# Local attention into a gated FFN: scores of both heads in row halves, and five PSUM banks shared by scores and V products

## The chip, the cores and the metric

One core of a Trainium2 chip. The metric is the device time of one execution in microseconds. TensorE (PE) multiplies into PSUM, ScalarE (ACT) and VectorE (DVE) read PSUM, GpSimd (POOL) works in SBUF and issues some of the DMAs, and SyncE (SP) issues the others. Each engine has its own list of instructions, and they wait for each other by semaphores.

## The reference

Attention with a local window of 96 keys and 8 global keys, then a gated FFN over all heads' outputs:

```python
scores = scale * q @ k.T                      # batch 4, heads 8, seq 768, head_dim 64
keep = (pos_k < 8) | ((rel >= 0) & (rel < 96))
dist = where(is_global & ~is_local, 96, abs(rel))
scores = where(keep, scores - slopes[h] * dist, -1e9)
a = exp(scores - max); a = a / (sum(a) + 1e-9)
x = (a @ v), heads side by side               # 3072 x 512
out = (maximum(x @ w_gate, 0) * (x @ w_val)) @ w_out   # 512 -> 1536 -> 512, float32
```

## The kernel before

**Halves and chunks.** The sequence of each batch is cut into two halves of 384 queries, so there are eight halves `s` = 0 to 7. Half `s` goes through attention, which leaves `xT` (512 features by 384 tokens), and chunk `c` = `s` of the FFN takes it from there. Halves 0 and 1 have code of their own (`scores`, `masks`, `first_sums` and so on); halves 2 to 7 are the "later halves", made by `attention_pieces`. Chunks 2 to 7 form the output product with seven products in place of eight for two of their three token tiles (`block`, sums in DVE).

**Attention of a later half**, for each of four head pairs `p` (two heads lie on the two halves of the 128 partitions):

- `early_pieces(s)`: POOL casts the loaded keys and queries to bf16 (`piece_cast_k`, `piece_cast_q`), SP issues transposing DMAs (`piece_xk` to `kN`, `piece_xq` to `qT`), and POOL puts the keys into steps of 128 (8 global and 120 local keys, `piece_order` with `put_keys`: three copies for each pair).
- Queries are padded: `qz` has, for each head, the head's 64 features and 64 zeros, so that `qT` holds both heads on all 128 rows and one product of 128 rows gives the scores of both heads side by side. Its zeros are written once (`Z`).
- `piece_qk(s, p, g)`, three for each pair: the scores of a group of key steps into one bank (`psum["qk"]`, three banks), an exp on ACT into `es`, and the mask products on DVE (L420).
- `piece_av(s, p, e)`, one for each head: V products into one bank (`psum["av"]`, two banks, L436); the same product with ones gives the sums; a Ln on ACT (L445), after the second head an Exp (L450) for the reciprocals and at once the two norms on DVE (L453).

**FFN of a chunk** (`ffn_pieces`): twelve times `gate` (L524, grelu on ACT, L531) and `val` (L524, product with grelu on DVE, L537), each in one of three `ff` banks, then the output products (L544, L583).

**What sets the order.** The program's text does: instructions enter each engine's list as they are issued. `weave` issues a list of FFN pieces and puts attention pieces between them at the places that `spread(items, first, last)` gives, as shares of the FFN list. The later halves begin like this, where chunk 0 is done but for its last third and chunk 1 has not begun:

```python
cast_k, x_k, cast_q, x_q, order_k = E[0:4], E[4:7], E[7:11], E[11:14], E[14:18]
for f in (*cast_k[:3], *cast_q[:3], lambda: nc.gpsimd.tensor_copy(held, wo_sb[0:1, N_FC - 1, 0:1]),
          cast_k[3], *x_k, cast_q[3], *x_q, lambda: spread_v_globals(1), *order_k):
    f()
...
weave(f1_1[G[0]])
```

`E` are the early pieces of half 2; `held` is a copy of one element that waits until the output weights `wo_sb` have been loaded. `weave(f1_1[G[0]])` issues the first four gates and values of chunk 1. Chunks 0 and 1 are then finished together with the attention of half 2; in chunk `c` of 2 to 6 the attention of half `c` + 1 is woven in.

Of the kernel before, what the change touches and what calls it, by code (L numbers as in the profile page):

```python
# [15 lines left out]
def kernel(  # L16
# [35 lines left out]
    banks_of_half = [[], []]  # L52
# [8 lines left out]
    banks_of_half[0] = [[by[0, 0]], [by[0, 1]], [by[0, 2], by[0, 3]]]  # L61
    banks_of_half[1] = [[by[1, 2], by[1, 5]], [by[1, 3], by[1, 6]], [by[1, 4]]]
# [31 lines left out]
    qTb = [const.tile([128, HP, 2, QH], BF16, name=f"qT{i}") for i in range(2)]  # L94
# [192 lines left out]
    def first_keys(p, copy_q):  # L287
        own = p < 2
        tps = [psum["t"].tile([128, 512], FP32, name="t_ps") for _ in range(1 + own)]
        tk = tps[0][:, 0 : QH // 2].bitcast(BF16)  # L290
        tq = tps[1][:, 0 : QH // 2].bitcast(BF16) if own else tps[0][:, QH // 2 : QH].bitcast(BF16)
        transposes(tk, cast_of[p][:, 0], cast_n)
        transposes(tq, cast_of[p][:, 1], cast_n)
        if own:
            put_keys(nc.vector.tensor_copy, nc.vector.tensor_copy, kT[0][p], tk, 0)
            copy_q(qTb[0][:, p, 0, :], tq)
        else:
            copy_q(qTb[0][:, p, 0, :], tq)
            put_keys(nc.vector.tensor_copy, nc.vector.tensor_copy, kT[0][p], tk, 0)

    def second_keys(p):
        tp = psum["t"].tile([128, 512], FP32, name="t_ps")
        tp = tp[:, 0:QH].bitcast(BF16).rearrange("d (i t) -> d i t", i=2)
        for i in range(2):
            transposes(tp[:, i], kq1[:, i, 2 * p : 2 * p + 2, :], load_n)
        nc.vector.tensor_copy(kNb[1][:, p], tp[:, 0])
        nc.vector.tensor_copy(qTb[1][:, p, 0, :], tp[:, 1])
        put_keys(nc.gpsimd.tensor_copy, nc.gpsimd.tensor_copy, kT[0][p], kNb[1][:, p], 1)
# [21 lines left out]
    def scores(s, p, g):  # L330
        half = s % 2
        spans_ = [by[half, j] for j in steps_of[half][g]]
        biased = half == 0 and 2 * p < NB
        if biased and (p, g) not in biased_of:
            distances(p, g)
        ps = biased_of[p, g] if biased else psum["s"].tile([128, 2, 512], FP32, name="s_ps")
        es = ef_pool.tile([128, 2, 360], BF16, name=f"ef{g}")
        cols = sum(NN * w for _, _, w, _ in spans_)
        qd = qTb[s][:, p, 0, :].rearrange("d (n t) -> d n t", n=NN)
        c = 0  # L340
        for i, (j, a, w, m) in enumerate(spans_):
            for e in range(2):
                r = slice(64 * e, 64 * e + 64)
                nc.tensor.matmul(ps[:, e, c : c + NN * w].rearrange("k (n t) -> k n t", n=NN),  # L344
                                 lhsT=kT[0][p][r, j, :], rhs=qd[r, :, a : a + w],
                                 start=(i == 0 and not biased), stop=(i == len(spans_) - 1),
                                 skip_group_check=True)
# [4 lines left out]
    def masks(s, p, g):  # L352
        for j in steps_of[s % 2][g]:
# [10 lines left out]
    def piece_cast_k(s, p):  # L364
        nc.gpsimd.tensor_copy(  # L365
            kc.rearrange("t n (h d) -> t h n d", d=D)[:, 2 * p : 2 * p + 2],
            ks_of[s][:, 2 * p : 2 * p + 2, :].rearrange("t e (n d) -> t e n d", n=NN))

    def piece_cast_q(s, p):

        qsrc = qs_of[s][:, 2 * p : 2 * p + 2, :].rearrange("t e (n d) -> t e n d", n=NN)
        for e in range(2):
            nc.gpsimd.tensor_copy(qz[:, :, p, e, 64 * e : 64 * e + 64], qsrc[:, e])  # L373

    def piece_xk(s, n):
        nc.sync.dma_start_transpose(
            out=kNb[s % 2][:, :, n * 128 : (n + 1) * 128], in_=kc[:, n])

    def piece_xq(s, n):
        nc.sync.dma_start_transpose(  # L380
            out=qTb[s % 2].rearrange("d p e t -> d (p e) t")[:, :, n * 128 : (n + 1) * 128],
            in_=qz[:, n].rearrange("t p e z -> t (p e z)"))

    def piece_order(s, p):
        b, half = divmod(s, 2)
        put_keys(nc.gpsimd.tensor_copy, nc.gpsimd.tensor_copy, kT[b % 2][p], kNb[s % 2][:, p], half)

    def early_pieces(s):
        out = [(0.0, lambda p=p: piece_cast_k(s, p)) for p in range(HP)]
        out += [(0.0, lambda n=n: piece_xk(s, n)) for n in range(NN)]  # L390
        out += [(0.0, lambda p=p: piece_cast_q(s, p)) for p in range(HP)]
        out += [(0.0, lambda n=n: piece_xq(s, n)) for n in range(NN)]
        out += [(0.0, lambda p=p: piece_order(s, p)) for p in range(HP)]
        return out

    def piece_qk(s, p, g):
        b, half = divmod(s, 2)
        kt = kT[b % 2][p]
        qd = qTb[s % 2][:, p].rearrange("d e (n p) -> d e n p", n=NN)
        bank = banks_of_half[half][g]  # L400
        cols = sum(2 * NN * w for _, _, w, _ in bank)
        ps = psum["qk"].tile([128, 512], FP32, name="qk_ps")
        most = max(sum(2 * NN * w for _, _, w, _ in of[g]) for of in banks_of_half)
        es = es_pool.tile([128, most], BF16, name=f"es{g}")
        c = 0
        for j, a, w, m in bank:
            n_ = 2 * NN * w
            nc.tensor.matmul(ps[:, c : c + n_], lhsT=kt[:, j, :],  # L408
                             rhs=qd[:, :, :, a : a + w], start=True, stop=True)
            c += n_  # L410
        nc.scalar.activation(es[:, 0:cols], ps[:, 0:cols], AF.Exp, bias=0.0, scale=scale)  # L411
        c = 0
        for j, a, w, m in bank:
            n_ = 2 * NN * w
            e4 = es[:, c : c + n_].rearrange("k (e n p) -> k e n p", e=2, n=NN)
            mk = m_all[:, 2 * p : 2 * p + 2, 0 if j == 0 else 1, :, m : m + w]
            if w == WQ:
                e4 = e4.rearrange("k e n p -> k e (n p)")
                mk = mk.rearrange("k e n p -> k e (n p)")
            nc.vector.tensor_mul(e4, e4, mk)  # L420
            es_of[s, p, j] = (es, c)
            c += n_

    def piece_av(s, p, e):
# [3 lines left out]
        av = psum["av"].tile([128, 512], FP32, name="av_ps")  # L428
        av_of[s, p, e] = av
        av3 = av[:, 0:QH].rearrange("d (n p) -> d n p", n=NN)  # L430
        todo = [t for bank in banks_of_half[half] for t in bank]
        for i, (j, a, w, m) in enumerate(todo):
            es, c = es_of[s, p, j]
            c += e * NN * w
# [3 lines left out]
                             rhs=es[:, c : c + NN * w].rearrange("k (n p) -> k n p", n=NN),  # L438
# [7 lines left out]
        if e == 1:  # L446
            if s not in xT_of:
                xT_of[s] = xt_pool.tile([128, N_DC, QH], BF16, name="xT")
            rc = rc_pool.tile([128, QH], FP32, name="rcp")
            nc.scalar.activation(rc, ln, AF.Exp, bias=0.0, scale=-1.0)  # L450
            for e_ in range(2):
                r = slice(64 * e_, 64 * e_ + 64)
                nc.vector.tensor_tensor(xT_of[s][r, p, :], av_of[s, p, e_][r, 0:QH], rc[r],  # L453
                                        op=ALU.mult)
# [45 lines left out]
    def attention_pieces(s, gaps=1):  # L500
        QK = lambda p: [(0.18, lambda g=g: piece_qk(s, p, g)) for g in range(3)]
        AV = lambda p: [(0.29, lambda e=e: piece_av(s, p, e)) for e in range(2)]
        g = QK(3)
# [11 lines left out]
    def ffn_pieces(c):  # L515
# [93 lines left out]
        def p2():  # L609
            ps = block("b", "qk", lambda i: cb[:, i, 1], lambda i: wo_sb[:, i, c0], True, True)  # L610
# [3 lines left out]
        def p5():  # L614
            ps = block("e", "qk", lambda i: cb[:, i, 0], lambda i: wo_sb[:, N2 + i, c1], True, True)
# [138 lines left out]
    qz = pool.tile([128, NN, HP, 2, 128], BF16, name="qz")  # L754
# [8 lines left out]
    def Z():  # L763
        nc.gpsimd.memset(qz.rearrange("t n p e z -> t (n p e z)").bitcast(mybir.dt.uint32), 0)
# [31 lines left out]
    ctx.enter_context(open_psum(ff=3, qk=3, av=2))  # L796
# [20 lines left out]
    for f in (*cast_k[:3], *cast_q[:3], lambda: nc.gpsimd.tensor_copy(held, wo_sb[0:1, N_FC - 1, 0:1]),  # L817
# [7 lines left out]
          spread(attention_pieces(2, 2), 0.46, 0.955), spread(early_pieces(3), 0.6, 0.92),  # L825
# [48 lines left out]
```

## Time and profile before

| | |
|---|---|
| time, median of 3 runs | 243.74 us (243.55 to 245.37) |
| profiled execution, its own time | 243.85 us |
| its span, first to last instruction | 242.1 us |
| PE busy | 235.5 us (97%) |
| DVE, ACT, POOL busy | 168.2, 151.4, 94.0 us |
| FFN gate and value products (L524) | 2 x 80 us, 768 products of 384 columns |
| scores of later halves (L408) | 25.0 us of matmul time, 108 products |
| their exps (L411) | 37.5 us, 72 of 527 ns |
| V products (L436) | 216 products |
| Ln, Exp, norms (L445, L450, L453) | 23.3, 12.6, 26.6 us |
| query casts (L373), key casts (L365) | 15.8 us in 48, 11.8 us in 24 |

How to read it: a matmul's duration is the time from its start to the modelled end of its results, and the next one starts earlier, so sums of matmul durations are larger than the time that they hold the engine. In a list of groups, the line is that of the kernel, then engine, operation, what it writes and reads, shapes and count; behind the bar stand the busy time in us and the mean of one in ns, then the engine's idle time before these instructions and what ended it. In a timeline a line has start and length in us.

### The profile page before, as it was taken

What the parts mean: (1) busy time and instruction counts of PE and PEld (TensorE: products, weight loads), DVE (VectorE), ACT (ScalarE), POOL (GpSimd) and SP (SyncE); (2) the same over time, 40 slices, a digit from 0 to 9 for tenths busy, and PEclk for the clock granted to TensorE, in tenths of its full rate; (3) what the DMA queues carried; (4) which work ended last, traced back from release to release, by engine and by line L of the source; (5) the groups of instructions that cost most, each with busy time, mean ns of one, the idle gap of its engine ahead of it and who ended that gap; (6) DMA issues with size and microseconds to landing.
All of it is one profiled execution on the core that took longest, in us unless ns stands there. A gap on an engine that the chain in (4) does not pass through costs nothing.

```text
span 242.1 us, 5085 instructions
## 1 busy us (share of the span) xinstructions
PE 235.5 (97%) x1810; PEld 148.9 (62%) x1819; DVE 168.2 (69%) x442; ACT 151.4 (63%) x316; POOL 94.0 (39%) x233
## 2 busy tenths in 40 slices
PE   7999999999999999999999999999999999999994
PEld 3655556555554666676667666676667666676663
DVE  7776864746774668777796679768796678765643
ACT  5898864333876787647864677637874587634330
POOL 6776992419448336802674067303530000000000
PEclk9999999999999999999999999999999999999999
DMA  6999999988999996878469868739591200020003
GB/s 199 183 196 178 251 232 222 183 107 131 283 213 175 224 232 116 106 151 266 80 123 123 248 166 152 50 123 270 98 101 43 91 0 0 3 109 21 3 17 113
DMA packets 79392, 33.75 MB, mean 139 GB/s; under 512 B 56952, under 2 KB 76408, under 8 KB 79368
## 3 DMA queue, kind: packets, MB, share of 16 engines
q1 hardware_dynamic: 46408, 23.82, 40.5%
q0 software_dynamic: 31744, 8.71, 34.7%
q10 hardware_dynamic: 1216, 0.92, 1.2%
q8 instruction: 14, 0.23, 0.4%
q14 instruction: 10, 0.08, 0.1%
HBM read 28.41 MB, written 6.29 MB: 143 GB/s over the span
## 4 chain that ended last, share of the span: by engine, by line
PE 91%; DVE 5%; ACT 2%; issue 1%
PE ff_ps L524 50%; PE ff_ps L544 11%; PE ff_ps L583 8%; PE av_ps L436 5%; PE qk_ps L408 5%; PE qk_ps L583 3%; PE t_ps L466 2%; DVE xT L453 2%; PE s_ps L344 2%; PE t_ps L275 2%; DVE es L420 1%; PE t_ps L678 1%; PE t_ps L313 1%; DVE ht L537 1%; ACT rcp L450 1%
## 5 line engine op out<-in xcount | busy, mean ns | idle before, releaser
L524 PE MATMUL ff_ps<-xT,wg 128*128 128x384 bf16 x384 | 80.2, 326 | 0.1
L524 PE MATMUL ff_ps<-xT,wv 128*128 128x384 bf16 x384 | 80.1, 326 | 0.0
L531 ACT ACTIVATE grelu<-ff_ps 128x384 bf16<-128x384 f32 x96 | 47.0, 489 | 36.0 <-DVE ht L537 20.2
L537 DVE TENSOR_TENSOR ht<-ff_ps,grelu 128x384 bf16<-128x384 f32 x96 | 53.1, 554 | 20.7 <-PE ff_ps L524 13.7
L411 ACT ACTIVATE es<-qk_ps 128x432 bf16<-128x432 f32 (+2 forms) x72 | 37.5, 527 | 20.9 <-PE qk_ps L408 20.1
L524 PEld LDWEIGHTS <-wv 128*128 128x128 bf16 x384 | 36.4, 97 | 22.9 <-issue 1.0
L524 PEld LDWEIGHTS <-wg 128*128 128x128 bf16 x384 | 35.5, 97 | 21.5 <-issue 0.7
L420 DVE TENSOR_TENSOR es<-es,m_all 128x432 bf16<-128x432 bf16 (+5 forms) x108 | 31.6, 322 | 14.3 <-ACT es L411 13.1
L453 DVE TENSOR_TENSOR xT<-av_ps,rcp 64x384 bf16<-64x384 f32 x48 | 26.6, 555 | 21.3 <-ACT rcp L450 20.4
L544 PE MATMUL ff_ps<-wo_sb,ht 128*128 128x512 bf16 x135 | 36.1, 378 | 0.5
L445 ACT ACTIVATE lnd<-av_ps 64x384 f32<-64x384 f32 x48 | 23.3, 485 | 16.4 <-PE av_ps L436 15.8
L365 POOL CAST kc<-ks 128x384 bf16<-128x384 f32 x24 | 11.8, 538 | 45.9 <-DMA ks<-in_k_dram 45.9
L408 PE MATMUL qk_ps<-qT,kT 128*128 128x432 bf16 (+5 forms) x108 | 25.0, 286 | 0.0
L436 PEld LDWEIGHTS <-vbuf 128*128 128x128 bf16 x216 | 18.2, 98 | 9.0 <-issue 1.2
L436 PE MATMUL av_ps<-es,vbuf 128*128 128x216 bf16 (+4 forms) x216 | 21.8, 226 | 1.1 <-DVE es L420 0.9
L140 POOL DMA_DIRECT2D vbuf<-in_v_dram x25 | 21.6, 877 | 2.0 <-DMA wv<-in_moe_w_val_dram 1.6
L373 POOL CAST qz<-qs 128x192 bf16<-128x192 f32 x48 | 15.8, 376 | 12.3 <-DMA qs<-in_q_dram 8.4
L544 PEld LDWEIGHTS <-ht 128*128 128x128 bf16 x144 | 12.9, 97 | 11.8 <-issue 0.5
L408 PEld LDWEIGHTS <-kT 128*128 128x128 bf16 x108 | 10.5, 98 | 8.2 <-POOL ks L169 0.4
L450 ACT ACTIVATE rcp<-lnd 128x384 f32<-128x384 f32 x24 | 12.6, 524 | 0.8
L350 ACT ACTIVATE ef<-s_ps 128x720 bf16<-128x720 f32 (+2 forms) x16 | 10.9, 710 | 2.0 <-PE s_ps L344 1.6
L266 POOL COPY kT<-kN 128x240 bf16<-128x240 bf16 x16 | 6.7, 416 | 8.7 <-DMA kN<-kc 6.6
(113 smaller groups left out, 239.9 us busy)
## 6 DMA issues: line engine op xcount, KB each, us to landing
out_dram<-osb SPq DMA_DIRECT2D x22, 256.0 KB, 4.2
ks<-in_k_dram SPq DMA_DIRECT2D x6, 768.0 KB, 5.8
qs<-in_q_dram SPq DMA_DIRECT2D x6, 768.0 KB, 8.0
vbuf<-in_v_dram POOLq DMA_DIRECT2D x21, 120.0 KB, 8.5
wg<-in_moe_w_gate_dram POOLq DMA_DIRECT2D x3, 512.0 KB, 9.0
wv<-in_moe_w_val_dram POOLq DMA_DIRECT2D x3, 512.0 KB, 10.2
wo_sb<-in_moe_w_out_dram POOLq DMA_DIRECT2D x1, 1536.0 KB, 20.7
kq<-in_q_dram ACTq DMA_DIRECT2D x2, 192.0 KB
```

The lines of the kernel that those rows point to most:

```text
L140: nc.gpsimd.dma_start(out=v_dst(b, NG + r0, NG + r0 + n, j), in_=v[b, :, KT * j + r0 : KT * j + r0 + n, :].rearrange("h p d -> p h d"))
L408: nc.tensor.matmul(ps[:, c : c + n_], lhsT=kt[:, j, :], rhs=qd[:, :, :, a : a + w], start=True, stop=True)
L411: nc.scalar.activation(es[:, 0:cols], ps[:, 0:cols], AF.Exp, bias=0.0, scale=scale)
L420: nc.vector.tensor_mul(e4, e4, mk)
L436: nc.tensor.matmul(av3[:, :, a : a + w], lhsT=vb[:, j, z0 : z0 + 128], rhs=es[:, c : c + NN * w].rearrange("k (n p) -> k n p", n=NN), star ...
L445: nc.scalar.activation(ln[o0 : o0 + 64], av[d0 : d0 + 64, 0:QH], AF.Ln, bias=0.0, scale=1.0)
L453: nc.vector.tensor_tensor(xT_of[s][r, p, :], av_of[s, p, e_][r, 0:QH], rc[r], op=ALU.mult)
L524: nc.tensor.matmul(st[key][:, 0:QH], lhsT=w_of(w, dc, fc), rhs=xT_of[c][:, dc, :], start=(dc == 0), stop=(dc == N_DC - 1))
L531: nc.scalar.activation(gr, psg[:, 0:QH], AF.Relu, bias=0.0, scale=1.0)
L537: nc.vector.tensor_tensor(ht[:, fc, :], psv[:, 0:QH], st["gr", fc], op=ALU.mult)
L544: nc.tensor.matmul(ps2, lhsT=ht[:, fc, n * 128 : (n + 1) * 128], rhs=wo_sb[:, fc, :], start=(fc == 0), stop=(fc == N_FC - 1))
L583: nc.tensor.matmul(st[key][:, 0:D2], lhsT=left(i), rhs=right(i), start=start and i == 0, stop=stop and i == N2 - 1, skip_group_check=not s ...
```

## The change

Scores of later halves: both heads' products are two matmuls of 64 rows each, one on each half of the partitions, into two banks; `pair_scores` issues all products of a head pair at once (four banks), and the exps and masks follow in the pieces behind (`pair_exps`, `masks`). The queries are transposed without padding (`qc` in place of `qz`). The pools `qk` (3) and `av` (2) become one pool `x` of five banks, which the output products of chunks 2 to 7 share. The norms are a piece of their own behind the V products (`piece_norm`), with an empty piece behind it. The places of attention and early pieces in the lists change slightly. The key copies of half 2 for head pairs 2 and 3 are made by ScalarE.

```diff
-    qTb = [const.tile([128, HP, 2, QH], BF16, name=f"qT{i}") for i in range(2)]
+    qTb = [const.tile([128, HP, QH], BF16, name=f"qT{i}") for i in range(2)]
...
-    def piece_cast_q(s, p):
-
-        qsrc = qs_of[s][:, 2 * p : 2 * p + 2, :].rearrange("t e (n d) -> t e n d", n=NN)
-        for e in range(2):
-            nc.gpsimd.tensor_copy(qz[:, :, p, e, 64 * e : 64 * e + 64], qsrc[:, e])
...
+    def piece_cast(s, p, of, to):
+        nc.gpsimd.tensor_copy(
+            to.rearrange("t n (h d) -> t h n d", d=D)[:, 2 * p : 2 * p + 2],
+            of[s][:, 2 * p : 2 * p + 2, :].rearrange("t e (n d) -> t e n d", n=NN))
+
+    def piece_x(s, n, data, out):
+        nc.sync.dma_start_transpose(out=out[:, :, n * 128 : (n + 1) * 128], in_=data[:, n])
 
     def piece_order(s, p):
         b, half = divmod(s, 2)
-        put_keys(nc.gpsimd.tensor_copy, nc.gpsimd.tensor_copy, kT[b % 2][p], kNb[s % 2][:, p], half)
+        copy = nc.scalar.copy if s == 2 and p >= 2 else nc.gpsimd.tensor_copy
+        put_keys(copy, copy, kT[b % 2][p], kNb[s % 2][:, p], half)
...
+    steps_later = [[(0, 3), (1, 2)], [(4, 2, 6), (3, 5)]]
+    banks_of = {}
+
+    def pair_scores(s, p):
+
+        half = s % 2
+        kt, qd = kT[s // 2 % 2][p], qTb[s % 2][:, p].rearrange("d (n t) -> d n t", n=NN)
+        for g in range(2):
+            banks = [psum["x"].tile([128, 512], FP32, name="x_ps") for _ in range(2)]
+            es = es_pool.tile([128, 2, 360], BF16, name=f"es{g}")
+            c = 0
+            for j, a, w, m in (by[half, j] for j in steps_later[half][g]):
+                for e in range(2):
+                    r = slice(64 * e, 64 * e + 64)
+                    nc.tensor.matmul(banks[e][:, c : c + NN * w].rearrange("k (n t) -> k n t", n=NN),
+                                     lhsT=kt[r, j, :], rhs=qd[r, :, a : a + w], start=True, stop=True)
+                es_of[s, p, j] = (es, c)
+                c += NN * w
+            banks_of[s, p, g] = banks, es, c
+
+    def pair_exps(s, p, g):
+        banks, es, c = banks_of[s, p, g]
+        for e in range(2):
+            nc.scalar.activation(es[:, e, 0:c], banks[e][:, 0:c], AF.Exp, bias=0.0, scale=scale)
+
     def piece_qk(s, p, g):
...
+        if g == 0:
+            pair_scores(s, p)
+        if g < 2:
+            pair_exps(s, p, g)
+        if g > 0:
+            masks(s, p, g - 1, steps_later)
...
-        av = psum["av"].tile([128, 512], FP32, name="av_ps")
+        av = psum["x"].tile([128, 512], FP32, name="x_ps")
...
+    def piece_norm(s, p):
+        for e in range(2):
+            r = slice(64 * e, 64 * e + 64)
+            nc.vector.tensor_tensor(xT_of[s][r, p, :], av_of[s, p, e][r, 0:QH], av_of[s, p, "r"][r],
+                                    op=ALU.mult)
...
-        return (QK(0) + QK(1) + AV(0) + QK(2) + AV(1) + g[0:1] + gap + a[0:1] + g[1:2] + a[1:2] + g[2:3]
-                + gaps * gap + AV(3))
+        return (QK(0) + QK(1) + AV(0) + N(0) + gap + QK(2) + AV(1) + N(1) + gap
+                + g[0:1] + a[0:1] + g[1:2] + a[1:2] + g[2:3] + N(2) + AV(3) + N(3))
...
-    qz = pool.tile([128, NN, HP, 2, 128], BF16, name="qz")
+    qc = pool.tile([128, NN, DM], BF16, name="qc")
...
-        nc.gpsimd.memset(qz.rearrange("t n p e z -> t (n p e z)").bitcast(mybir.dt.uint32), 0)
...
-    ctx.enter_context(open_psum(ff=3, qk=3, av=2))
+    ctx.enter_context(open_psum(ff=3, x=5))
...
-          spread(attention_pieces(2, 2), 0.46, 0.955), spread(early_pieces(3), 0.6, 0.92),
+          spread(attention_pieces(2), 0.38, 0.93), spread(early_pieces(3), 0.58, 0.9),
...
-            placed.append(spread(attention_pieces(c + 1), *((0.06, 0.8) if c == 2 else (0.0, 0.78))))
+            placed.append(spread(attention_pieces(c + 1), *((0.02, 0.8) if c == 2 else (0.0, 0.8))))
```

More of the change, by code (lines that the diff above doesn't have):

```diff
@@ L49 @@
     assert QH == NN * 128 and WQ * NN >= KT + NL - 1
-    banks_of_half = [[], []]
     spans = []
@@ L60 @@
     by = {(h_, j): (j, a, w, m) for h_, j, a, w, m in spans}
-    banks_of_half[0] = [[by[0, 0]], [by[0, 1]], [by[0, 2], by[0, 3]]]
-    banks_of_half[1] = [[by[1, 2], by[1, 5]], [by[1, 3], by[1, 6]], [by[1, 4]]]
     const = ctx.enter_context(tc.tile_pool(name="const", bufs=1))
@@ L295, in first_keys @@
             put_keys(nc.vector.tensor_copy, nc.vector.tensor_copy, kT[0][p], tk, 0)
-            copy_q(qTb[0][:, p, 0, :], tq)
+            copy_q(qTb[0][:, p], tq)
         else:
-            copy_q(qTb[0][:, p, 0, :], tq)
+            copy_q(qTb[0][:, p], tq)
             put_keys(nc.vector.tensor_copy, nc.vector.tensor_copy, kT[0][p], tk, 0)
@@ L306, in second_keys @@
         nc.vector.tensor_copy(kNb[1][:, p], tp[:, 0])
-        nc.vector.tensor_copy(qTb[1][:, p, 0, :], tp[:, 1])
+        nc.vector.tensor_copy(qTb[1][:, p], tp[:, 1])
         put_keys(nc.gpsimd.tensor_copy, nc.gpsimd.tensor_copy, kT[0][p], kNb[1][:, p], 1)
@@ L338, in scores @@
         cols = sum(NN * w for _, _, w, _ in spans_)
-        qd = qTb[s][:, p, 0, :].rearrange("d (n t) -> d n t", n=NN)
+        qd = qTb[s][:, p].rearrange("d (n t) -> d n t", n=NN)
         c = 0
@@ L350, in scores, with masks @@
         nc.scalar.activation(es[:, :, 0:cols], ps[:, :, 0:cols], AF.Exp, bias=0.0, scale=scale)
-    def masks(s, p, g):
-        for j in steps_of[s % 2][g]:
+    def masks(s, p, g, steps=steps_of):
+        for j in steps[s % 2][g]:
             _, a, w, m = by[s % 2, j]
@@ L362, in masks @@
             nc.vector.tensor_mul(for_all, for_all, mk)
-    def piece_cast_k(s, p):
+    def piece_cast(s, p, of, to):
         nc.gpsimd.tensor_copy(
-            kc.rearrange("t n (h d) -> t h n d", d=D)[:, 2 * p : 2 * p + 2],
-            ks_of[s][:, 2 * p : 2 * p + 2, :].rearrange("t e (n d) -> t e n d", n=NN))
-    def piece_cast_q(s, p):
-        qsrc = qs_of[s][:, 2 * p : 2 * p + 2, :].rearrange("t e (n d) -> t e n d", n=NN)
-        for e in range(2):
-            nc.gpsimd.tensor_copy(qz[:, :, p, e, 64 * e : 64 * e + 64], qsrc[:, e])
@@ L375, in piece_xk @@
[L375 to L382, printed above, removed]
+            to.rearrange("t n (h d) -> t h n d", d=D)[:, 2 * p : 2 * p + 2],
+            of[s][:, 2 * p : 2 * p + 2, :].rearrange("t e (n d) -> t e n d", n=NN))
@@ L384, in piece_order @@
+    def piece_x(s, n, data, out):
+        nc.sync.dma_start_transpose(out=out[:, :, n * 128 : (n + 1) * 128], in_=data[:, n])
     def piece_order(s, p):
         b, half = divmod(s, 2)
-        put_keys(nc.gpsimd.tensor_copy, nc.gpsimd.tensor_copy, kT[b % 2][p], kNb[s % 2][:, p], half)
+        copy = nc.scalar.copy if s == 2 and p >= 2 else nc.gpsimd.tensor_copy
+        put_keys(copy, copy, kT[b % 2][p], kNb[s % 2][:, p], half)
     def early_pieces(s):
-        out = [(0.0, lambda p=p: piece_cast_k(s, p)) for p in range(HP)]
@@ L390, in early_pieces @@
-        out += [(0.0, lambda n=n: piece_xk(s, n)) for n in range(NN)]
-        out += [(0.0, lambda p=p: piece_cast_q(s, p)) for p in range(HP)]
-        out += [(0.0, lambda n=n: piece_xq(s, n)) for n in range(NN)]
+        out = [(0.0, lambda p=p: piece_cast(s, p, ks_of, kc)) for p in range(HP)]
+        out += [(0.0, lambda n=n: piece_x(s, n, kc, kNb[s % 2])) for n in range(NN)]
+        out += [(0.0, lambda p=p: piece_cast(s, p, qs_of, qc)) for p in range(HP)]
+        out += [(0.0, lambda n=n: piece_x(s, n, qc, qTb[s % 2])) for n in range(NN)]
@@ L393, in early_pieces @@
         out += [(0.0, lambda p=p: piece_order(s, p)) for p in range(HP)]
         return out
-    def piece_qk(s, p, g):
[L397 to L422, printed above, removed]
@@ L427, in piece_av @@
         vb = vbuf[b % 2]
-        av = psum["av"].tile([128, 512], FP32, name="av_ps")
+        av = psum["x"].tile([128, 512], FP32, name="x_ps")
         av_of[s, p, e] = av
         av3 = av[:, 0:QH].rearrange("d (n p) -> d n p", n=NN)
-        todo = [t for bank in banks_of_half[half] for t in bank]
+        todo = [by[half, j] for g in steps_later[half] for j in g]
         for i, (j, a, w, m) in enumerate(todo):
             es, c = es_of[s, p, j]
-            c += e * NN * w
             z0 = 2 * D * h + (D if e == 0 else 0)
@@ L437, in piece_av @@
                              lhsT=vb[:, j, z0 : z0 + 128],
-                             rhs=es[:, c : c + NN * w].rearrange("k (n p) -> k n p", n=NN),
+                             rhs=es[:, e, c : c + NN * w].rearrange("k (n p) -> k n p", n=NN),
                              start=(i == 0), stop=(i == len(todo) - 1),
@@ L448, in piece_av @@
                 xT_of[s] = xt_pool.tile([128, N_DC, QH], BF16, name="xT")
-            rc = rc_pool.tile([128, QH], FP32, name="rcp")
+            rc = av_of[s, p, "r"] = rc_pool.tile([128, QH], FP32, name="rcp")
             nc.scalar.activation(rc, ln, AF.Exp, bias=0.0, scale=-1.0)
[L451 to L454, printed above, removed]
+    def piece_norm(s, p):
[3 more added lines that the diff above has]
+                                    op=ALU.mult)
     def first_sums(s, p, what, tile_=None):
@@ L498, in first_norm, with attention_pieces @@
         first_product(s, p)
-    def attention_pieces(s, gaps=1):
-        QK = lambda p: [(0.18, lambda g=g: piece_qk(s, p, g)) for g in range(3)]
+    def attention_pieces(s):
+        QK = lambda p: [(0.15, lambda g=g: piece_qk(s, p, g)) for g in range(3)]
         AV = lambda p: [(0.29, lambda e=e: piece_av(s, p, e)) for e in range(2)]
+        N = lambda p: [(0.0, lambda: piece_norm(s, p))]
         g = QK(3)
@@ L609, in p2 @@
         def p2():
-            ps = block("b", "qk", lambda i: cb[:, i, 1], lambda i: wo_sb[:, i, c0], True, True)
+            ps = block("b", "x", lambda i: cb[:, i, 1], lambda i: wo_sb[:, i, c0], True, True)
             V2(st["r", 1][:, c0], ps, st["r", 0][:, c0], op=ALU.add)
@@ L614, in p5 @@
         def p5():
-            ps = block("e", "qk", lambda i: cb[:, i, 0], lambda i: wo_sb[:, N2 + i, c1], True, True)
+            ps = block("e", "x", lambda i: cb[:, i, 0], lambda i: wo_sb[:, N2 + i, c1], True, True)
             V2(st["r", 0][:, c1], ps, st["r", 0][:, c1], op=ALU.add)
```

## The prediction

> **What bounds the kernel now.** I read the busy table first, then the windows by stage, then the chain that ended last.
>
> ```profile
> PE 235.5 (97%) x1810; PEld 148.9 (62%) x1819; DVE 168.2 (69%) x442; ACT 151.4 (63%) x316; POOL 94.0 (39%) x233
> ```
>
> ```profile
> 56.57:77.73 21.16, 20.29 (x119) 10.52 (x121) 12.78 (x32) 14.32 (x30) 13.45 (x36) 1.00 1.09 206
> ...
> 133.41:161.31 27.90, 27.80 (x211) 18.61 (x210) 21.32 (x54) 18.62 (x40) 10.77 (x27) 1.00 0.70 143
> ```
>
> The first line gives each engine's busy time. In the windows the columns after the length are PE, PEld, DVE, ACT and POOL. PE is full in every stage, the other engines have a quarter of their time free or more. So PE time that is taken away shortens the run, work added to ACT, DVE or POOL is hidden, and any time in which PE has nothing to do is added whole. The chain that ended last agrees: PE has 91% of it.
>
> The timeline around the point where attention data of half 2 is prepared matters most here (start, length, engine, line; in brackets the idle time before):
>
> ```profile
> 34.44 0.49 ACT L531 ACTIVATE grelu<-ff_ps 128x384 bf16<-128x384 f32 x1
> 35.77 0.81 PE L524 MATMUL ff_ps<-xT,wg 128*128 128x384 bf16 x4
> 36.42 0.81 PE L524 MATMUL ff_ps<-xT,wv 128*128 128x384 bf16 x4
> 36.62 0.49 ACT L531 ACTIVATE grelu<-ff_ps 128x384 bf16<-128x384 f32 x1 [1.69 <-PE ff_ps L524]
> 37.07 0.81 PE L524 MATMUL ff_ps<-xT,wg 128*128 128x384 bf16 x4
> 37.72 0.65 PE L524 MATMUL ff_ps<-xT,wv 128*128 128x384 bf16 x3
> ```
>
> ```profile
> 47.58 0.18 POOL L817 COPY held<-wo_sb 1x1 bf16<-1x1 bf16 x1 [1.96 <-DMA wo_sb<-in_moe_w_out_dram]
> 47.71 0.50 POOL L365 CAST kc<-ks 128x384 bf16<-128x384 f32 x1
> ...
> 54.00 0.54 POOL L262 COPY kT<-kN 128x360 bf16<-128x360 bf16 x1 [5.22 <-DMA kN<-kc]
> ...
> 58.51 0.09 POOL L169 MEMSET qs<- 1x1 f32 x1
> ```
>
> Chunk 1's first gate product starts at 35.77 and its first grelu at 36.62. The transposed keys of half 2 (kN) land only at 54.0: POOL is held until the output weights have landed (47.58), casts the last keys, and then three transposing DMAs run. While POOL waits for kN, everything queued behind waits too, even the 1x1 memset at 58.51, which reads no keys.
>
> **The change, part by part.**
>
> 1. *Two of the four key orderings of half 2 move from POOL to ACT.* `piece_order` takes nc.scalar.copy for s == 2, p >= 2: three copies for each p, six in all. These pieces are issued in the list that stands before `weave(f1_1[G[0]])`, and in the built order of ACT's instructions the six stand directly behind the grelu that is the one at 34.44, the first of them waits for the three kN transposes, and behind it stand the 16 grelus that in the old trace run from 36.62 to 56.12. ACT reaches that wait at 34.9 and leaves it when kN lands. Nothing that decides this landing changes: the wo_sb load, `held`, the last key cast and the three key transposes keep their order, and the casts of the first six query heads, though they shrink, were waiting for data before and are done before 47.58. So ACT goes on at 54.0.
>
>  The copies: from the exp rows below, 336 columns take 448 ns and 480 take 567, so 0.826 ns a column and 170 fixed. 360, 24 and 56 columns give 468 + 190 + 217 = 875 ns, twice 1.75. The first grelu of chunk 1 starts at 55.75 and ends at 56.24. PE meanwhile fills the three ff buffers (g0, v0, g1: 35.77, 36.42, 37.07) and must wait for the first of them before v1, which started at 37.72. It starts at about 56.3. **Delay 18.6 us**, and PE, which is full from there to the end, cannot take any of it back. Bounds: 17.5, if PE ran further or kN landed 1 us earlier because less else is in transfer, to 19.5.
>
> ```profile
> L411 ACT ACTIVATE es<-qk_ps 128x432 bf16<-128x432 f32 x36 | 18.8, 527 | 12.1 <-PE qk_ps L408 11.8
> L411 ACT ACTIVATE es<-qk_ps 128x480 bf16<-128x480 f32 x24 | 13.4, 567 | 7.7 <-PE qk_ps L408 7.2
> L411 ACT ACTIVATE es<-qk_ps 128x336 bf16<-128x336 f32 x12 | 5.4, 448 | 1.1 <-PE qk_ps L408 1.1
> ```
>
>  What POOL gains (the orderings of p 2 and 3, 56 to 58.5) is nothing that PE waits for later.
>
> 2. *TensorE after a long pause.* PE would stand idle from about 37.9 to 56.3. The trace has no pause like it inside the run; its start is the nearest row. The first seven 512-column products took 3.17 us together, 0.453 each, where three such products take 0.65 later, 0.217 each:
>
> ```profile
> 1.28 3.17 PE t_ps L678 x7
> ...
> 58.99 0.65 PE ff_ps L544 x3
> ```
>
>  These seven alone lose 3.17 - 7 x 0.217 = 1.65 us, and products at the longer time go on until about 7 us from the start: 5.9 us at half rate would be 2.95 lost. If an idle PE inside the run does not lose its rate, 0. I take **+2.2**, between the two that the trace shows.
>
>  The Trainium skill ("TensorE: Matmul & The Clock Gate", Part 1) says that the array's clock falls to half after an idle window of 3.4 us and comes back after about 3.4 us of work. By it the loss would be some 1.7 us, as an estimate, and the sum 0.5 us lower, 262.0. The start of this trace shows a longer slow stretch than that, and no row here shows a pause of such length inside the run.
>
> 3. *Scores in row halves.* Old: one product for each key step, both heads side by side over the padded queries, 1200 columns a head pair in even halves, 1392 in odd ones. A steady group of 4 x 384 columns takes 0.65 us, 0.423 ns a column: 0.51 and 0.59 us. New: two products for each step, one on each half of the rows, 600 and 696 columns each, if they run side by side. The early scores (L344) already have this form; these lines show an odd half, all ten products:
>
> ```profile
> 26.42 0.76 PE ff_ps L524 x4
> 27.18 0.41 PE s_ps L344 x10
> 27.59 0.76 PE ff_ps L524 x4
> ```
>
>  They do run side by side, but the group of four around them takes 0.76 in place of 0.65. So 0.41 + 0.11 = 0.52 against 0.59: 0.07 gained. Of the 0.52, 696 x 0.423 = 0.29 is streaming and 0.23 is changing over; an even half costs 0.25 + 0.23 = 0.48 against 0.51: 0.03 gained. Twelve head pairs of each kind: **-1.2 us**. Bounds: 0 (the early even half of eight products, 0.43 in the chain, with 0.11 is no better than 0.51) to -1.9 (two thirds more).
>
> 4. *Exps and masks.* Four exps a head pair in place of three. Even: 2 x 368 + 2 x 468 = 1.67 against 2 x 527 + 448 = 1.50; odd: 2 x 448 + 2 x 468 = 1.83 against 2 x 567 + 527 = 1.66. So 24 x 0.17 = 4.1 us more on ACT, where each chunk of some 27 us has 8 us or more free: 0. If ACT filled up in 56 to 77 (14.3 of 21.2 busy), it would be 0.7 us. Mask products keep their count and columns: 0.
>
> 5. *Unpadded queries.* Query casts: 24 of 0.54 us (the key casts' row) in place of 48 of 0.376, and a 1.4 us memset goes; the query transposes move half. POOL and the SP queue are covered by PE everywhere: 0. Without that cover, half 3's data would be late at 77; but item 1's delay leaves its transfers 18 us more.
>
> 6. *Five shared PSUM banks, norms a place later.* A score piece takes four banks at once; the next pair needs a bank that the exps and, from the third pair on, the norm of an earlier pair must free. In exchange, DVE reaches a norm when its reciprocal is ready. Old waits to be had: the line of the V products (L436) shows 1.1 us of PE idle, the stage 56.57 to 77.73 another few tenths. New waits to be feared: one of the old size (0.4 us) in each of six halves, 2.4. I take **-0.8** (half a microsecond or so kept), bounds -1.5 to +2.4.
>
> Sum: 242.1 + 18.6 + 2.2 - 1.2 - 0.8 = 260.9 span. The profiled execution took 243.85 for its 242.1, and the median is 243.74, so 1.64 is added: **262.5 us**.
>
> **The rivals.**
>
> *A. No slow restart*, everything else as above: 260.3. For it: nothing but the start shows the slow rate. Against it: the same idle-then-work pattern is just what the start is.
>
> *B. Bank waits on top*: the four-bank demand stops PE in each half, +2.4 where I have -0.8: 265.7. For it: five banks of which scores want four; against it: the gap and the later norm leave more than 2 us between a norm and the score piece that needs its bank.
>
> *C. The six copies stop nothing* (the other side). If ACT passed them in time, only items 3 and 6 are left: 243.74 - 1.2 - 0.8 = 241.7, faster. It decides if kN has landed when ACT gets there, which must be before about 37.5; then ACT's two free microseconds before 36.62 take the copies. Against it: 54.0 in the trace, and a wait that is written into the first copy. Only a second, earlier arrival of wo_sb, q and k together could do this, and DMA is full from 20 to 47 us.
>
> *D. The stall is shorter*, because the load of the output weights lands some microseconds earlier now that a 1.4 us memset no longer stands behind it in POOL's queue and the V loads start earlier. The memset stands behind wo_sb's issue, so it can't hasten it; even 3 us would only give 259.5.
>
> **How the numbers follow.** My forecast (with A and D as its near variants) 0.86, B 0.09, C 0.04; 0.01 for other things. Range: from 258.5 (A with the full gain of items 3 and 6, and kN half a microsecond earlier) to 266 (B). About 1% can be told from no change in this kernel (three runs before: 243.55 to 245.37). Faster by over 1% comes from C alone, some of which ends within 1%: 0.03 and 0.02; slower: 0.95.
>
> **What would show it.** Right: ACT idle from about 35 to 54 in front of a kT copy that ended on DMA kN, no PE work from 38 to 56, products at about twice their time for some 3 to 6 us after it, then a chunk with even-half attention of about 27.0 us, with odd 27.5. The 384-column products after an x_ps score should show the 0.11 longer group. Wrong: kT copies of ACT that run before 40, or a chunk longer than now by more than 0.5 us, which would mean bank waits; a total under 250 would mean that the first item is wrong as a whole.

## The result and the profile after

The changed kernel takes 260.75 us (median of 4 runs, 259.89 to 262.25), the kernel before 243.65 in the runs beside it: a ratio of 1.069, 95% interval 1.062 to 1.077. The forecast was 262.5, range 258.5 to 266.0. The profiled execution spans 259.7 us.

The page's busy table, the PE and PE clock rows of its 40 slices (6.5 us each), and one of its groups:

```profile
PE 234.8 (90%) x1918; PEld 144.7 (56%) x1927; DVE 168.2 (65%) x442; ACT 154.0 (59%) x346; POOL 85.8 (33%) x202
...
PE   7989990039999999999999999999999999999995
PEclk9999997559999999999999999999999999999999
...
L259 ACT COPY kT<-kN 128x360 bf16<-128x360 bf16 x2 | 1.1, 542 | 18.4 <-DMA kN<-kc 18.4
```

PE is as busy as before, but over 17.6 us more. Slices 7 and 8 (39 to 52 us) hold no PE work at all, and the granted clock falls to half there and is still at half when work begins again. The group says who stood still first: ScalarE waited 18.4 us in front of its key copies for the transposed keys.

The timeline of ScalarE, then of TensorE, at that place:

```profile
35.22 0.49 ACT L524 ACTIVATE grelu<-ff_ps 128x384 bf16<-128x384 f32 x1
54.12 0.54 ACT L259 COPY kT<-kN 128x360 bf16<-128x360 bf16 x1 [18.41 <-DMA kN<-kc]
...
55.56 0.86 ACT L524 ACTIVATE grelu<-ff_ps 128x384 bf16<-128x384 f32 x2
```

```profile
37.85 0.81 PE L517 MATMUL ff_ps<-xT,wg 128*128 128x384 bf16 x4
56.09 1.44 PE L517 MATMUL ff_ps<-xT,wv 128*128 128x384 bf16 x4 [17.42 <-ACT grelu L524]
57.33 1.48 PE L517 MATMUL ff_ps<-xT,wg 128*128 128x384 bf16 x4
58.60 1.27 PE L517 MATMUL ff_ps<-xT,wv 128*128 128x384 bf16 x4
59.71 0.81 PE L517 MATMUL ff_ps<-xT,wg 128*128 128x384 bf16 x4
```

Read the two together. After the grelu at 35.22 ScalarE has nothing that it may do until 54.12. TensorE fills the three ff buffers, the last with the products at 37.85, and then waits 17.4 us for a grelu. Three groups of four then take 3.62 us up to 59.71, where three take 1.95 at the later pace of 0.65: 1.67 us of slow restart.

Later, away from the pause, a chunk is a little shorter than before. Two windows, each one chunk, with an even and an odd half's attention in it:

```profile
124.58:151.50 26.92, 26.87 (x215) 17.46 (x214) 20.23 (x51) 18.34 (x44) 11.78 (x25) 1.00 0.76 137
151.50:179.15 27.65, 27.57 (x231) 17.88 (x230) 21.80 (x55) 18.99 (x44) 10.10 (x23) 1.00 0.66 130
```

The first stands against 27.10 in the kernel before (106.31 to 133.41 there), the second against the 27.90 of the window shown in the prediction.

### The profile page after: what moved, and what is told of

Read it like the earlier page. It is cut to its first block, busy times and chain, and to the rows that moved or that the text cites. A ratio compares the mean times of both kernels' runs of the same rounds, so it can differ in the third digit from the quotient of the medians.

```text
span 259.7 us, 5334 instructions
## 1 busy us (share of the span) xinstructions
PE 234.8 (90%) x1918; PEld 144.7 (56%) x1927; DVE 168.2 (65%) x442; ACT 154.0 (59%) x346; POOL 85.8 (33%) x202
## 4 chain that ended last, share of the span: by engine, by line
PE 77%; DMA 13%; DVE 3%; POOL 2%; ACT 2%; SPq 1%; issue 1%; ACTq 0%; DVEq 0%
PE ff_ps L517 45%; PE ff_ps L537 11%; DMA wo_sb<-in_moe_w_out_dram 8%; PE ff_ps L576 8%; PE x_ps L426 5%; DMA kq<-in_q_dram 4%; PE x_ps L396 4%; PE x_ps L576 3%; PE t_ps L671 1%; DMA kN<-kc 1%; SPq L367 1%; PE t_ps L272 1%; POOL wv L155 1%; POOL wg L155 1%; DVE ef L359 0%
## 5 line engine op out<-in xcount | busy, mean ns | idle before, releaser
L517 PE MATMUL ff_ps<-xT,wv 128*128 128x384 bf16 x384 | 81.3, 329 | 18.0 <-ACT grelu L524 17.4
L405 ACT ACTIVATE es<-x_ps 128x360 bf16<-128x360 f32 (+2 forms) x96 | 36.8, 444 | 19.4 <-PE x_ps L396 19.3
L359 DVE TENSOR_TENSOR es<-es,m_all 128x432 bf16<-128x432 bf16 (+4 forms) x108 | 31.4, 336 | 10.0 <-ACT es L405 9.5
L537 PE MATMUL ff_ps<-wo_sb,ht 128*128 128x512 bf16 x135 | 34.7, 379 | 0.6 <-issue 0.2
L445 DVE TENSOR_TENSOR xT<-x_ps,rcp 64x384 bf16<-64x384 f32 x48 | 26.6, 554 | 10.3 <-ACT rcp L440 9.6
L435 ACT ACTIVATE lnd<-x_ps 64x384 f32<-64x384 f32 x48 | 23.3, 485 | 12.1 <-PE x_ps L426 11.5
L426 PE MATMUL x_ps<-es,vbuf 128*128 128x216 bf16 (+4 forms) x216 | 22.0, 225 | 0.4 <-DVE xT L445 0.3
L426 PEld LDWEIGHTS <-vbuf 128*128 128x128 bf16 x216 | 15.8, 97 | 8.4 <-DVE xT L445 0.5
L362 POOL CAST qc<-qs 128x384 bf16<-128x384 f32 x24 | 11.7, 526 | 10.7 <-DMA qs<-in_q_dram 7.4
L259 ACT COPY kT<-kN 128x360 bf16<-128x360 bf16 x2 | 1.1, 542 | 18.4 <-DMA kN<-kc 18.4
L396 PE MATMUL x_ps<-qT,kT 64*128 64x216 bf16 (+4 forms) x216 | 11.1, 224 | 0.0
```

The costliest lines, as they stand in the source:

```text
L362: nc.gpsimd.tensor_copy(to.rearrange("t n (h d) -> t h n d", d=D)[:, 2 * p : 2 * p + 2], of[s][:, 2 * p : 2 * p + 2, :].rearrange("t e (n ...
L405: nc.scalar.activation(es[:, e, 0:c], banks[e][:, 0:c], AF.Exp, bias=0.0, scale=scale)
L426: nc.tensor.matmul(av3[:, :, a : a + w], lhsT=vb[:, j, z0 : z0 + 128], rhs=es[:, e, c : c + NN * w].rearrange("k (n p) -> k n p", n=NN), s ...
L435: nc.scalar.activation(ln[o0 : o0 + 64], av[d0 : d0 + 64, 0:QH], AF.Ln, bias=0.0, scale=1.0)
L445: nc.vector.tensor_tensor(xT_of[s][r, p, :], av_of[s, p, e][r, 0:QH], av_of[s, p, "r"][r], op=ALU.mult)
L517: nc.tensor.matmul(st[key][:, 0:QH], lhsT=w_of(w, dc, fc), rhs=xT_of[c][:, dc, :], start=(dc == 0), stop=(dc == N_DC - 1))
```

## The experiments

### All orderings on POOL

```diff
-        copy = nc.scalar.copy if s == 2 and p >= 2 else nc.gpsimd.tensor_copy
+        copy = nc.gpsimd.tensor_copy
```

> All of the change but the six key copies on ScalarE: all four key orderings of half 2 are again on POOL. Theory (the wait at the head of ScalarE's list is the whole loss): the TensorE pause of 17.4 us and the slow restart of 1.7 us vanish, 260.75 - 17.6 - 1.7 = 241.5 us, ratio to before 0.991. Rival (the row halves or the shared banks cost as well): 244 or more. Rival (the copies only uncover a lateness of the keys): a pause remains at about 56 to 58 in front of the first scores, 243 to 250.

Measured: 241.97 us, ratio to before 0.992 (0.990 to 0.994). The pause and the slow restart are gone, as the PE and PE clock rows of its page show:

```profile
PE   7998999999999999999999999999999999999994
...
PEclk9999999999999999999999999999999999999999
```

The rest of the change is worth 0.8%, about 1.9 us, and this version beats both kernels.

### ScalarE's copies alone, in the kernel before

```diff
-        put_keys(nc.gpsimd.tensor_copy, nc.gpsimd.tensor_copy, kT[b % 2][p], kNb[s % 2][:, p], half)
+        copy = nc.scalar.copy if s == 2 and p >= 2 else nc.gpsimd.tensor_copy
+        put_keys(copy, copy, kT[b % 2][p], kNb[s % 2][:, p], half)
```

> The kernel before with that one part of the change alone: the key orderings of head pairs 2 and 3 of half 2 by ScalarE. Theory: TensorE pauses from about 38 to 56 as in the changed kernel and restarts slowly, 243.65 + 17.6 + 1.7 = 263.0 us, a little over the changed kernel's 260.75, since the gains of the other parts are missing. Rival (it takes the shared banks or the unpadded data to make the loss): within 2 us of 243.65.

Measured: 264.07 us, ratio 1.083 (1.078 to 1.087). One line, put into the old kernel, makes the whole loss. In its profile TensorE pauses 17.9 us, and the restart is longer than in the changed kernel: five groups take 6.16 us in place of 3.25.

```profile
55.68 1.44 PE L525 MATMUL ff_ps<-xT,wv 128*128 128x384 bf16 x4 [17.93 <-ACT grelu L532]
```

### The same work on ScalarE, later in its list

```diff
-              cast_k[3], *x_k, cast_q[3], *x_q, lambda: spread_v_globals(1), *order_k):
+              cast_k[3], *x_k, cast_q[3], *x_q, lambda: spread_v_globals(1), *order_k[:2]):
...
+          [(0.34, order_k[2]), (0.36, order_k[3])],
```

> The whole change, with ScalarE's six copies woven in at 0.34 and 0.36 of the third list of FFN pieces, where the old trace is at about 55 us, in place of ahead of chunk 1. ScalarE does the same work. Theory (place in the list, not the work): no pause, 241.5 us, the same as with all orderings on POOL within 0.5. Rival (ScalarE's extra work costs): 243 or more.

Measured: 242.29 us, ratio 0.993 (0.991 to 0.995): the same as with all orderings on POOL, within the intervals. ScalarE makes all six copies, from 55.2 to 57.3, and nothing waits for them. TensorE does stand once, in front of the first scores of half 2:

```profile
58.12 0.45 PE L396 MATMUL x_ps<-qT,kT 64*128 64x216 bf16 x8 [1.44 <-issue]
```

These are scores of head pair 0, whose keys POOL puts in order; what they wait for comes up below, with the banks and norms. So it is the place in the list that costs, not the engine nor the work.

### The wait without the work

```diff
+              lambda: nc.scalar.copy(held3, kNb[0][0:1, 2, 0:QH:128]), *order_k):
```

(with all orderings on POOL)

> All four key orderings on POOL, but at the old place ScalarE copies three elements of the transposed keys, so that it waits for the same three landings and does next to no work. Theory (the wait is the loss): the pause is 17.4 less the 1.44 us of the six copies, plus 0.2 for the small one: 260.75 - 1.2 = 259.5 us. Rival (the copies themselves are the loss): 241.5 us.

Measured: 259.32 us, ratio 1.063 (1.058 to 1.068). ScalarE's timeline, then TensorE's:

```profile
53.08 0.20 ACT L812 COPY held<-kN 1x3 bf16<-1x3 bf16 x1 [18.00 <-DMA kN<-kc]
```

```profile
53.70 1.44 PE L517 MATMUL ff_ps<-xT,wv 128*128 128x384 bf16 x4 [15.68 <-ACT grelu L524]
```

A copy of three elements stops TensorE for 15.7 us. ScalarE's next grelu starts 0.1 us behind it, where the six copies put 1.44 us between the landing and the grelu; the two kernels' times lie 1.4 us apart. The wait is all the rest.

### The keys land later

```diff
+              *[lambda: nc.gpsimd.tensor_copy(held_more, held_more2)] * 8, cast_k[3], *x_k, cast_q[3], *x_q, lambda: spread_v_globals(1), *order_k):
```

> The whole change with ScalarE's copies as they are, and eight copies of 384 columns on POOL (some 0.5 us each, their result is not used) between the copy that waits for the output weights and the last key cast, so that the key transposes start 4 us later. Theory (the pause of TensorE lasts to the landing of the transposes): 4 us more, 260.75 + 4.0 = 264.8 us, with ScalarE's first key copy at 58 in place of 54. Rival (the pause is ended by something else): 260.75.

Measured: 265.46 us, ratio 1.088 (1.083 to 1.092). ScalarE, then TensorE:

```profile
58.57 0.55 ACT L259 COPY kT<-kN 128x360 bf16<-128x360 bf16 x1 [22.81 <-DMA kN<-kc]
```

```profile
60.54 1.44 PE L517 MATMUL ff_ps<-xT,wv 128*128 128x384 bf16 x4 [21.83 <-ACT grelu L524]
```

The eight copies took 4.47 us on POOL, the first key copy came 4.45 us later, TensorE went on 4.45 us later, and the whole took 4.7 us more. So the landing ends the pause, one for one. An earlier landing wasn't tried, nor a TensorE kept busy through the pause.

### What a pause costs behind it

A kernel of its own, run once: `products(n)` makes n products of 384 columns into one bank, ScalarE copies between them hold TensorE up.

```python
ps = products(60)
for n in (1, 2, 4, 6, 8, 10, 14, 20, 38, 38, 6, 8):
    for _ in range(n):
        nc.scalar.copy(t, ps[:, 0:384])
    ps = products(44)        # the first of them reads t
```

> None of the reference's computation: TensorE runs 60 products of 384 columns, then twelve times it waits for a row of ScalarE copies (1, 2, 4, 6, 8, 10, 14, 20, 38, 38, 6 and 8 of some 0.45 us each) and runs 44 products; the output is a copy of some weights. It measures by itself what a pause costs behind it. Theory (an idle TensorE loses its rate after a few microseconds and has it back after a few of work): behind pauses under about 3 us products stand 162 ns apart, behind those of 4 us and more 10 to 21 of them stand 320 ns apart, as many behind 17 us as behind 5. Rival (the loss grows with the pause): more of them behind 17 us than behind 5. Rival (the eleven long products in the changed kernel were long for another reason): 162 ns behind all pauses.

TensorE's timeline: the first product behind a pause with the idle time before it, then the other 43 with the time that they took.

```profile
24.83 0.32 PE L33 MATMUL g_ps<-t,w 128*128 128x384 bf16 x1 [1.13 <-ACT t L40]
24.99 7.15 PE L33 MATMUL g_ps<-w 128*128 128x384 bf16 x43
34.30 0.32 PE L33 MATMUL g_ps<-t,w 128*128 128x384 bf16 x1 [2.15 <-ACT t L40]
34.46 8.83 PE L33 MATMUL g_ps<-w 128*128 128x384 bf16 x43
...
141.26 0.48 PE L33 MATMUL g_ps<-t,w 128*128 128x384 bf16 x1 [19.53 <-ACT t L40]
141.54 8.53 PE L33 MATMUL g_ps<-w 128*128 128x384 bf16 x43
```

Pauses of 0.57 and 1.13 us cost nothing behind them (7.15 us). The pause of 2.15 us costs 1.68, the ones of 3.2 to 19.5 us between 1.4 and 2.8, with no trend by length: the two pauses of 19.53 us stand at 8.53 and 9.71. So the restart has a price that does not grow with the pause, and it varies by a factor of two. The expected threshold of 3 us was wrong: 2.15 us was enough here.

The granted clock shows what sets the price. In each of the traces with a pause its changes lie whole multiples of 3.41 us apart, wherever the program's work begins or ends in between. Three windows, each from the first product behind a pause to the return of the full clock: behind the two pauses of 19.53 us, and in the changed kernel. The clock, 0.50, stands behind the five engines.

```profile
141.26:144.33 3.07, 3.06 (x10) 1.46 (x10) 0.00 (x0) 0.00 (x0) 0.00 (x0) 0.50 0.00 0
169.60:175.05 5.45, 5.45 (x18) 2.58 (x18) 0.00 (x0) 0.00 (x0) 0.00 (x0) 0.50 0.01 3
```

```profile
56.09:59.52 3.43, 3.43 (x11) 1.57 (x11) 1.10 (x2) 0.82 (x2) 2.47 (x3) 0.50 0.89 94
```

About half of each length is lost: 1.5, 2.7 and 1.7 us. In these traces each such step of 3.41 us at full clock in which products ran for under 0.4 of the time was followed by half the clock, and each with 0.46 or more was not; back from half the clock, a step with 0.84 was enough and one with 0.74 was not. So it is where a pause falls on these steps that sets its price, and for a short one also whether there is a price.

The Trainium skill ("TensorE: Matmul & The Clock Gate", Part 1) says that the clock halves after an idle window of about 3.4 us, whose phase runs freely, and comes back after about as much work. One such window at half rate, 1.7 us lost as an estimate, lies inside the measured 1.4 to 2.8, and the steps of 3.41 us agree with the window. The pause of 2.15 us that sufficed here is shorter than the window, so the window need not be idle throughout: the measurement decides.

### Banks and norms alone, first at the new places, then at the old

The kernel before with `open_psum(ff=3, x=5)` and `piece_norm`; padded queries, one product for both heads:

```diff
-    ctx.enter_context(open_psum(ff=3, qk=3, av=2))
+    ctx.enter_context(open_psum(ff=3, x=5))
...
-            for e_ in range(2):
-                r = slice(64 * e_, 64 * e_ + 64)
-                nc.vector.tensor_tensor(xT_of[s][r, p, :], av_of[s, p, e_][r, 0:QH], rc[r],
-                                        op=ALU.mult)
+    def piece_norm(s, p):
...
+        return (QK(0) + QK(1) + AV(0) + N(0) + gap + QK(2) + AV(1) + N(1) + gap
+                + g[0:1] + a[0:1] + g[1:2] + a[1:2] + g[2:3] + N(2) + AV(3) + N(3))
```

> The kernel before with the shared pool of five banks, the norms as a piece of their own and the new places alone; padded queries, one product for both heads and all orderings on POOL stay. It splits what is left of the change. Theory by the prediction's sum: 243.65 - 0.8 = 242.85 us, and the row halves' 1.2 to 1.5 us stand between this and the change with the orderings on POOL. Rival (the gain all comes from the banks and norms, the row halves give nothing because of the changing over): 241.5. Rival (the new places cost in the old form): 244 or more.

Measured: 244.84 us, ratio 1.004 (1.002 to 1.006): slower, where 0.8 us less was expected. TensorE's timeline shows two waits in front of first scores, of half 2 and of half 3:

```profile
59.45 0.34 PE L408 MATMUL x_ps<-qT,kT 128*128 128x432 bf16 x1 [1.38 <-POOL ks L169]
...
80.84 0.36 PE L408 MATMUL x_ps<-qT,kT 128*128 128x144 bf16 x2 [0.49 <-DMA qT<-qz]
```

The second names its cause: the padded query transposes. For the first, POOL's memset is only the last thing that happened by then. The time speaks for the same cause: the last query transpose had been issued by 57.5 and the score starts 1.9 us later, as in the kernel before (56.75 and 58.65). With unpadded queries it is 1.3 us in both runs that wait there: 56.4 and 57.7 with all orderings on POOL, 56.8 and 58.1 with ScalarE's copies later. So the new places bring the first scores ahead of their queries, and unpadded queries land in time, or nearly.

With the attention of halves 2 and 3 at the old places (that of the later halves keeps the slightly changed ones):

```diff
-          spread(attention_pieces(2), 0.38, 0.93), spread(early_pieces(3), 0.58, 0.9),
+          spread(attention_pieces(2), 0.46, 0.955), spread(early_pieces(3), 0.6, 0.92),
...
-            placed.append(spread(attention_pieces(c + 1), *((0.02, 0.8) if c == 2 else (0.0, 0.8))))
+            placed.append(spread(attention_pieces(c + 1), *((0.06, 0.8) if c == 2 else (0.0, 0.8))))
```

> The five shared banks and the norms as pieces of their own, alone, with padded queries, one product for both heads and the orderings on POOL, and with the attention of halves 2 and 3 at the places of the kernel before (0.46 to 0.955, 0.06 to 0.8). With the new places this form had waited 1.5 us at 57.5 and 0.65 us at 79.8 in front of first scores, whose padded queries land late. Theory (banks and norms bring the old 0.4 to 0.7 us waits of V products away, the places cost in the padded form): 243.96 - 0.8 = 243.2 us. Rival (banks and norms bring nothing): 244 or more.

Measured: 242.52 us, ratio 0.994 (0.992 to 0.996). Banks and norms alone are worth about 1.5 us, twice what was expected. What TensorE's V products waited for, in the list of waits of the kernel before and of this one (total us, times, longest):

```profile
PE av_ps L436 <- DVE es L420: 0.9, 2, 0.5
```

```profile
PE x_ps L436 <- DVE es L420: 0.2, 1, 0.2
```

The list counts only what the modelled ends leave visible. By the starts of TensorE's products, those at 70.25, 75.21, 100.52 and 146.87 in the old kernel come 0.38, 0.66, 0.57 and 0.20 us later than the products before them need, in or just behind V products, 1.8 us in all; in this one two V products from 74.98 on come 0.44 us late together. The difference of 1.4 us is nearly all that was measured.

### A later start for half 2

```diff
-          spread(attention_pieces(2), 0.38, 0.93), spread(early_pieces(3), 0.58, 0.9),
+          spread(attention_pieces(2), 0.45, 0.95), spread(early_pieces(3), 0.58, 0.9),
```

(with all orderings on POOL)

> The change with all key orderings on POOL and the attention of half 2 spread over 0.45 to 0.95 of its list in place of 0.38 to 0.93. With the orderings on POOL the first scores waited 0.3 us at 57 (1.5 us in the run with ScalarE's copies placed later), and the only data that land so late are the query transposes of half 2. Theory (the first scores now come ahead of their queries): the wait goes, 241.97 - 0.3 = 241.6 us. Rival (fewer FFN pieces between attention pieces make new waits for exps and norms): 242.3 or more.

Measured: 241.67 us, ratio 0.990 (0.988 to 0.993). The wait in front of the first scores of half 2 is gone from the profile; those of half 3 now wait 0.3 us for their query transposes. Against the same version with the earlier start the difference of 0.3 us lies inside the intervals.

### Scores behind the chunk's first gate

```diff
-            placed.append(spread(attention_pieces(c + 1), *((0.02, 0.8) if c == 2 else (0.0, 0.8))))
+            placed.append(spread(attention_pieces(c + 1), 0.04, 0.8))
```

(with the later start for half 2)

> The change with all key orderings on POOL, the attention of half 2 spread over 0.45 to 0.95, and in chunks 2 to 6 the attention places over 0.04 to 0.8, so that the first scores of a half come behind the chunk's first gate and value in place of ahead of the first gate's grelu. In the run with 0.0 to 0.8 TensorE stood 0.18 us at each odd half's begin for an ff bank whose grelu was queued behind two exps. Theory (four exps a head pair crowd the first grelu): some 0.2 us less in up to four chunks, 241.67 - 0.6 = 241.1 us. Rival (the wait only moves to a later grelu): 241.7.

Measured: 243.21 us, ratio 0.998 (0.995 to 1.001): the gain is gone. The waits of 0.18 us that were to go are gone too, but in the list of waits one line is new, and a chunk with an even half's attention takes 27.4 us in place of 26.9:

```profile
PE x_ps L396 <- DVE xT L445: 1.0, 4, 0.4
```

```profile
105.18:132.60 27.42, 27.12 (x215) 17.55 (x215) 20.45 (x51) 18.36 (x44) 11.55 (x25) 1.00 0.76 135
```

A score piece waits for a bank that a norm must still free, four times as the list counts them, up to 0.4 us each; by the starts of the products it is five times, 0.30 to 0.54 us, 1.9 us in all. It is the mechanism of the prediction's rival B. The changed kernel has it once, in half 2, where the first V product behind the last scores waits:

```profile
PE x_ps L426 <- DVE xT L445: 0.3, 1, 0.3
```

Otherwise it just escapes it: pieces closer by 5% are enough to bring it about in each of the next halves.

## Why the prediction was right

The forecast lies 1.75 us above the measured median. In the profiled execution the span was 259.7 us where 260.9 was forecast: 0.23 of this is item 1, 0.53 item 2, and 0.44 the other parts, which brought 2.4 us in that execution where 2.0 was forecast.

**Item 1, the wait at the head of ScalarE's list**, carried the forecast, and each step of it was seen. The keys land at 54.1 (54.0 forecast), v1 goes on at 56.09 (56.3), so the delay is 18.4 us (18.6). Chunk 1 itself began 0.8 us later in this execution, and that changed nothing, since the landing sets the end. The copies took 1.44 us, not 1.75: they overlap, and from start to start it is 0.45, 0.13 and 0.14 us, less than the line through the exps' durations gave. The copies alone in the old kernel, the same copies later, and the three-element wait leave no room for another cause.

**Item 2, the restart**: 2.2 forecast, 1.67 in the profiled execution, 1.4 to 2.9 in the other runs with a pause. It is not one number: in the changed kernel the full clock came back 3.43 us after TensorE's first product behind the pause, with the copies alone in the old kernel 5.94 us after it. The forecast had no step for this, and that it came within 0.53 us is in part luck. This is part of why the changed kernel's runs lie between 259.9 and 262.3; the longest has a mean clock of 0.959, the other three of 0.967.

**Item 3, row halves**: 1.2 us forecast. In the trace a score block, changing over included, holds TensorE 0.474 us in an even half and 0.507 in an odd one, against 0.51 and 0.59: 12 x (0.036 + 0.083) = 1.4 us. Not all of it arrives. In odd halves TensorE stands 0.18 us early in the chunk, because the first grelu, which frees an ff buffer, is queued behind two of the four exps. Item 4 priced those exps at nothing, and this is where they cost a little. The chunk with an odd half takes 27.65 us where 27.5 was forecast, the one with an even half 26.92 for 27.0. The row halves were not run alone: from the banks and norms alone (242.52) to the change without ScalarE's copies (241.97) some 0.5 us are left for them, the unpadded queries and the places together.

**Item 6, banks and norms**: 0.8 forecast, 1.5 measured alone. Its error and that of item 3 nearly cancel, which is luck: together the two were to bring 2.0 us, and the change without ScalarE's copies brings 1.9.

**Item 5, unpadded queries**, was costed at nothing, with POOL and SP covered. The old kernel's first score of half 2 already started just as its queries could be there, so the earlier places of the change need the smaller transposes: the padded form at the new places lost 2.3 us against the same form at the old ones.

**The rivals.** A (no slow restart) is refuted by the clock row. B happened once in this kernel, 0.3 us in place of the 2.4 that it feared, and more of it is near, as the last experiment shows. C and D are out: the copies stopped everything, and the wo_sb load landed no earlier (48.2 in place of 47.6).

## What to carry to other kernels

An instruction that waits for a DMA belongs in an engine's list where the DMA has landed, not where its code happens to stand. Before moving work to another engine, read in the old timeline when its input lands, and what that engine would have started in between: here 18 us of grelus behind six copies of 0.2 to 0.5 us each. When a change is a bundle, undo the one line with the strange wait first; the other parts were a gain of 0.8% all the time.

## What the runs showed of the hardware

A TensorE pause of 2.15 us was enough to halve the granted clock; one of 1.13 us was not, nor the 1.44 us in the run with the copies placed later. After the 2.15 us pause the products first ran at full rate for 0.8 us (162 ns from start to start), then ten came 320 ns apart: the lower clock can set in after the pause is over. The clock changed only at steps of 3.41 us, by how much of a step TensorE had worked. The price behind a pause, 1.4 to 2.9 us, does not depend on its length from 2 to 20 us.

Going from products on all 128 rows to products on row halves, and back, costs 0.09 to 0.10 us each way in every score block of the trace. Of the 0.25 us of streaming that an even half's block saves (600 columns at 0.423 ns), some 0.2 go back into it.
